# Gated linear attention with a feed-forward block: a chunk's 24 state products on four column groups instead of three

## The chip, the cores and the metric

The kernel runs on one core of a Trainium2 chip. The metric is the device time of one execution in microseconds. The core's engines are TensorE (PE, with its weight loads shown apart as PEld), VectorE (DVE), ScalarE (ACT), GpSimd (POOL), and SyncE (SP), which issues most of the transfers. TensorE's array can be used as four groups of 32 columns; a product in a group writes the 32 partitions of the accumulator (PSUM) that belong to the group.

## The reference

Everything is float32. First comes an attention block with complex gates, for 4 batches, 8 heads, 768 time steps and a head width of 48; then a feed-forward block over the 3072 rows that it leaves.

```python
mag = np.sqrt(a_re * a_re + a_im * a_im)
scale = np.minimum(mag, 0.999) / (mag + 1e-06)
a_re_n, a_im_n = (a_re * scale, a_im * scale)
for t in range(S):
    ar, ai = (a_re_n[:, :, t, :, None], a_im_n[:, :, t, :, None])
    new_re = ar * S_re - ai * S_im
    new_im = ar * S_im + ai * S_re
    kv = np.einsum('bhd,bhe->bhde', k[:, :, t], v[:, :, t])
    S_re, S_im = (new_re + kv, new_im)
    y[:, :, t] = np.einsum('bhd,bhde->bhe', q[:, :, t], S_re)
...
x = np.ascontiguousarray(attn_out.transpose(0, 2, 1, 3)).reshape(B * S, H * D)
a = x @ w1
b = x @ w2
h = a * b @ w3
return (h @ w_out).astype(np.float32)
```

## The kernel before

The product of w3 and w_out is formed once at the start (`fuse`), so the feed-forward block is two products with w1 and w2, their elementwise product `ab`, and one product with the fused matrix `w3o`.

The attention is cut into 8 units: 4 batches of two halves of 384 steps, each of three chunks of 128 steps, with all 8 heads in a unit. For each unit the gates are turned into running magnitudes and angles (on ScalarE and VectorE, tiles `gA`, `gR`, `gZ`, `re`, `im`), q and k are scaled and rotated by them, and the results are moved by transfers into `QL` and `KL`, whose partitions hold 96 rows per head (48 real, 48 imaginary). Then come, chunk by chunk:

- `turn` (L984): transposes of the scaled k on TensorE into `tp`, copied by ScalarE to `KT`. A chunk has two, for the real and the imaginary part.
- `state` (L1060): the state of 96 rows by 48 columns for each head, as a product of `KT` and v. The 96 rows are three blocks of 32, so a chunk has 8 heads times 3 blocks, 24 products, each with all 128 partitions in, 32 columns of weights and 48 columns moving. They stand in the tile `kv`, with block g of every head on column group g. The sum with the chunk before goes into a tile `T` (three of them take turns): one VectorE addition for all heads (L1075), or one ScalarE copy at a batch's first chunk (L1073). At the end of a unit's third chunk a second VectorE operation (L1078) multiplies the state by a gate. A batch needs five states, so 20 stages run in all: 4 with the copy and 16 with the addition.
- `scores` (L995): the products of `KL` and `QL` into two accumulator tiles `sc`, four column groups, with 128, 32, 96 and 64 columns; VectorE copies them with a mask into `A` (L1007).
- `outputs` (L1018): `A` with v, and `QL` with the state `T`, into `y`. From unit 2 on, `y` is split into three parts `x`, by ScalarE (L1047), VectorE (L1050) and POOL (L1051).

`tp`, `kv` and `y` share a pool of two accumulator tiles, `ps_v` (L464): a new one needs the one before last to be read out.

The feed-forward products of the unit before (`m` at L1089, `o` at L1184, evicted at L1101, L1105, L1123, L1130 and L1188) fill TensorE between these pieces. TensorE's order is written out by `pieces` (L1489) and `unit` (L1519). The gate steps of the next unit are placed between them on VectorE and ScalarE by a planner: `run` (L1579) keeps a clock for each engine, charges each piece of work by a table `TIMES` (L1536), and puts a step where it thinks that it fits. The first 36 places are fixed by a list (L441). The same clocks decide how many inspections of the raw inputs (`look`, from L1264: a load, then three to five operations on POOL) go ahead of the `x` operations in POOL's queue; the loads of the next unit's k, q and v stand behind the `x` operations in that queue. A fallback for unusual inputs, at the head of the file, isn't run here.

## Time and profile before

| what | us |
| --- | --- |
| three timed runs | 534.25, 535.98, 538.77 |
| their median | 535.98 |
| span of the profiled execution, first to last instruction (its only time on record) | 534.5 |
| a state stage's 48 records on TensorE, along the chain | 0.81 to 0.88 |
| addition of a state, L1075, mean of 16 | 0.549 |
| copy of a state, L1073, median of 4 | 0.466 |

The profile shows two records for each float32 product, so a stage of 24 products is "x48". Its rows by tile:

```profile
L1069 PEld LDWEIGHTS kv<-vr,KT x960: 106/110/110, 59.3 to 461.7; 128*32 128x32 f32 x192
L1069 PE MATMUL kv<-vr,KT x960: 206/206/231, 59.3 to 461.7; 128*32 128x48 f32 x192
L1073 ACT COPY T<-kv x4: 458/466/477, 61.2 to 396.7; 96x384 f32<-96x384 f32 x4
```

The columns are the shortest, median and longest duration in ns, the first and last start in us, and the form. A single record takes 206 ns from end to end, but a stage of 48 takes under 0.9 us, since records on different column groups overlap and successive ones are pipelined. A row of the page's groups has the line, engine, operation, output and inputs with their shapes and the count, then busy time, mean ns and idle time ahead of the engine. A row of a timeline or of the chain has its start and its length first. "x" after the tile names is a count; x as a name is the split output.

### The profile page before, as it was taken

How to read it: one execution, taken by the hardware profiler on the slowest of the kernel's cores; microseconds unless marked ns; L12 is line 12 of the kernel's file. 1: busy time of each engine (PE TensorE's matmuls, PEld its weight loads, DVE VectorE, ACT ScalarE, POOL GpSimd, SP SyncE). 2: the span in 40 equal slices, each digit the busy share in tenths (PEclk: the TensorE clock that was granted, in tenths of full speed). 3: DMA queues.
4: the chain of work that ended last, by engine and by line, in shares of the span. 5: the costliest groups of instructions: out<-in, count | busy, mean ns of one | idle time of the engine just before them, and what ended most of it. 6: DMA issues, size and time to landing. Idle time of an engine off the chain costs nothing.

```text
span 534.5 us, 13643 instructions
## 1 busy us (share of the span) xinstructions
PE 498.3 (93%) x5594; PEld 378.1 (71%) x5594; DVE 374.7 (70%) x607; ACT 325.6 (61%) x569; POOL 254.0 (48%) x317
## 2 busy tenths in 40 slices
PE   5689889999998999988999999999999998999995
PEld 2355565556655679957888688967896787878972
DVE  7999699855779988756773876577657837336750
ACT  6979866665675458982587557855786554213420
POOL 1000000028968886752664765487457458415510
PEclk9899999999999999998999999999999999999999
DMA  8999859692379219791599239932993176716611
GB/s 258 369 400 286 189 161 307 126 232 72 79 174 229 73 56 234 157 219 40 126 236 216 77 82 245 225 90 70 229 232 87 40 209 169 205 43 189 200 50 37
DMA packets 66424, 89.75 MB, mean 168 GB/s; under 512 B 29872, under 2 KB 53872, under 8 KB 65584
## 3 DMA queue, kind: packets, MB, share of 16 engines
q1 hardware_dynamic: 57904, 59.15, 44.0%
q0 software_dynamic: 8448, 29.63, 20.3%
q8 instruction: 46, 0.75, 0.6%
q14 instruction: 26, 0.21, 0.1%
HBM read 61.01 MB, written 4.72 MB: 123 GB/s over the span
## 4 chain that ended last, share of the span: by engine, by line
PE 51%; DVE 17%; DMA 13%; issue 6%; ACT 5%; POOL 5%; SPq 1%; POOLq 0%; DVEq 0%; ACTq 0%
PE m L1089 24%; PE o L1184 16%; PE y L1043 4%; PE sc L1004 4%; DMA k<-in_k_dram 3%; DMA KL<-k 3%; PE kv L1069 2%; DVE gR L750 2%; PE tp L991 2%; DMA QL<-q 2%; DMA q<-in_q_dram 2%; DMA look<-in_a_re_dram 1%; DVE gA L753 1%; DMA raw<-in_w_dram 1%; POOL look L1327 1%
## 5 line engine op out<-in xcount | busy, mean ns | idle before, releaser
L1184 PE MATMUL o<-w3o,ab 128*128 128x384 f32 x384 | 131.7, 492 | 0.0
L1089 PE MATMUL m<-x,low 128*128 128x384 f32 x576 | 119.2, 339 | 0.0
L1089 PEld LDWEIGHTS m<-x,low 128*128 128x128 f32 x576 | 102.6, 188 | 0.2 <-ACT m L1123 0.2
L1184 PEld LDWEIGHTS o<-w3o,ab 128*128 128x128 f32 x384 | 70.4, 190 | 45.6 <-issue 2.4
L1105 DVE TENSOR_TENSOR ab<-m,ab 128x384 f32<-128x384 f32 x64 | 35.1, 553 | 57.2 <-PE m L1089 39.4
L1089 PE MATMUL m<-x,wh 128*128 128x384 f32 x288 | 69.6, 350 | 3.4 <-ACT ab L1130 2.4
L1123 ACT ACTIVATE m<-m 128x384 f32<-128x384 f32 x96 | 45.5, 476 | 36.0 <-PE m L1089 35.6
L1089 PE MATMUL m<-xT,ws 128*128 128x384 f32 x192 | 63.1, 487 | 1.2 <-ACT xT L1054 1.2
L1328 POOL TENSOR_SCALAR look<-look 128x192 f32<-128x192 f32 (+1 forms) x55 | 54.4, 988 | 5.0
L1089 PEld LDWEIGHTS m<-x,wh 128*128 128x128 f32 x288 | 50.8, 188 | 7.4 <-ACT ab L1130 3.6
L1325 POOL TENSOR_TENSOR look<-look 128x256 f32<-128x256 f32 (+1 forms) x43 | 31.9, 743 | 50.1 <-DMA look<-in_w_dram 32.3
L1089 PEld LDWEIGHTS m<-xT,ws 128*128 128x128 f32 x192 | 36.0, 190 | 25.6 <-ACT xT L1054 1.7
L1273 POOL MEMSET seen<- 128x256 bf16 x1 | 0.3, 317 | 107.7 <-DVE ab L1105 107.7
L1007 DVE COPY_PREDICATED A<-mask,sc 128x512 f32<-128x512 uint8 x48 | 32.8, 734 | 26.5 <-PE sc L1004 26.5
L1289 POOL TENSOR_TENSOR seen<-seen,look 128x192 bf16<-128x192 bf16 (+1 forms) x55 | 44.3, 805 | 4.5
L1051 POOL TENSOR_TENSOR x<-x,x 128x384 fp32r<-128x384 f32 x18 | 23.1, 1284 | 41.7 <-DVE x L1050 41.5
L1188 ACT COPY ot<-o 128x384 f32<-128x384 f32 x24 | 11.4, 476 | 48.4 <-PE o L1184 48.2
L1043 PE MATMUL y<-A,V 128*32 128x128 f32 x768 | 40.2, 276 | 0.6 <-issue 0.6
L1004 PEld LDWEIGHTS sc<-QL,KL 96*32 96x32 f32 x1536 | 29.2, 112 | 13.6 <-issue 8.7
L1004 PE MATMUL sc<-QL,KL 96*32 96x32 f32 (+3 forms) x1536 | 32.8, 238 | 4.4 <-DMA QL<-q 3.0
L1043 PEld LDWEIGHTS y<-A,V 128*32 128x32 f32 x768 | 35.0, 112 | 1.5 <-issue 1.5
L1043 PE MATMUL y<-QL,T 96*32 96x128 f32 x640 | 35.6, 275 | 0.0
(163 smaller groups left out, 909.2 us busy)
## 6 DMA issues: line engine op xcount, KB each, us to landing
looked<-in_w_dram POOLq DMA_DIRECT2D x14, 512.0 KB, 4.5
look<-in_w_dram POOLq DMA_DIRECT2D x27, 256.0 KB, 5.0
raw<-in_w_dram SPq DMA_DIRECT2D x6, 1024.0 KB, 10.3
KL<-gR SPq DMA_DIRECT2D x24, 192.5 KB, 3.6
KL<-k SPq DMA_DIRECT2D x24, 192.5 KB, 7.1
QL<-gA SPq DMA_DIRECT2D x24, 192.0 KB, 8.2
QL<-q SPq DMA_DIRECT2D x24, 192.0 KB, 7.9
raw<-in_w_dram SPq DMA_DIRECT2D x6, 768.0 KB, 6.1
```

The lines of the kernel that those rows point to most:

```text
L1004: nc.tensor.matmul(out=sc[SB * g:SB * g + SB, j, s0:C], lhsT=KL[:, x * n + j, w][:, s0:s0 + SB], rhs=QL[:, x * n + j, w][:, s0:C], start=T ...
L1007: last["sc", u, c, x] = nc.vector.copy_predicated(out=A[:, x * n:(x + 1) * n], data=sc, mask=mask)
L1043: nc.tensor.matmul(out=o, lhsT=a, rhs=b, start=s0, stop=s1)
L1051: nc.gpsimd.tensor_tensor(out=x[2], in0=x[1], in1=x[0], op=OP.subtract)
L1089: nc.tensor.matmul(out=out, lhsT=a, rhs=b, start=start and i == 0, stop=i == len(terms) - 1, skip_group_check=not start)
L1105: last["ab", u, j] = nc.vector.tensor_tensor(out=ab_t[u][:, j], in0=m, in1=ab_t[u][:, j], op=OP.mult)
L1123: nc.scalar.activation(out=got[m], in_=got[m], func=AF.Copy, scale=1.0 + 1.0 / BITS)
L1184: nc.tensor.matmul(out=m, lhsT=ab_t[u][:, f, t * P:(t + 1) * P], rhs=w3o[:, f], start=(f == 0), stop=(f == KF - 1))
L1188: nc.scalar.copy(out=o, in_=m)
L1289: nc.gpsimd.tensor_tensor(out=seen[:, 0:n], in0=seen[:, 0:n], in1=x, op=OP.add)
L1325: tt(out=x, in0=x, in1=x, op=OP.mult)
L1328: ts(out=x, in0=x, scalar1=low, scalar2=None, op0=OP.is_ge)
```

## The change

`kv` gets all 128 partitions. Heads 0 to 5 keep their places on column groups 0 to 2. The six products of heads 6 and 7 (two heads by three blocks) go to the fourth group, partitions 96 to 127: head slots 0 and 1 there hold block 0 of heads 6 and 7, slots 2 and 3 hold block 1, slots 4 and 5 block 2. So the 24 products are issued as six times four. What is summed is the same; since the blocks of heads 6 and 7 now lie on other partitions than their rows of `T`, the sum is written as four operations: heads 0 to 5 on 96 partitions, and three of 32 partitions and two heads, each from partitions 96 to 127 into its block. The same holds for the ScalarE copies. The table `TIMES` gets new costs for these three kinds of piece.

```diff
-        kv = ps_v.tile([2 * D, H, D], FP, tag="v", name="kv")
-        for hd in range(H):
-            rows = KT[:, hd].rearrange("p d x f -> p (d x f)")
+        kv = ps_v.tile([P, H, D], FP, tag="v", name="kv")
+        fits, spare = H - H // LANES, 3 * SB
+        for hd in range(fits):
             for g in range(0, 2 * D, SB):
+                rows = KT[:, hd].rearrange("p d x f -> p (d x f)")
                 nc.tensor.matmul(out=kv[g:g + SB, hd], lhsT=rows[:, g:g + SB], rhs=V[:, hd], start=True, stop=True)
+            g, over = divmod(hd, H - fits)
+            rows = KT[:, fits + over].rearrange("p d x f -> p (d x f)")
+            nc.tensor.matmul(out=kv[spare:spare + SB, hd], lhsT=rows[:, SB * g:SB * g + SB], rhs=V[:, fits + over],
+                             start=True, stop=True)
         Tn = Tb[(u * UC + c) % 3]
+        areas = [(slice(0, 2 * D), slice(0, 2 * D), slice(0, fits), slice(0, fits))]
+        areas += [(slice(SB * g, SB * g + SB), slice(spare, spare + SB), slice(fits, H), slice(g * (H - fits), (g + 1) * (H - fits)))
+                  for g in range(3)]
         with tc.high_priority():
-            if T is None:
-                nc.scalar.copy(out=Tn[:, :, 0:D], in_=kv)
-            else:
-                nc.vector.tensor_tensor(out=Tn[:, :, 0:D], in0=kv, in1=T[:, :, 0:D], op=OP.add)
+            for rows, lanes, heads, slots in areas:
+                if T is None:
+                    nc.scalar.copy(out=Tn[rows, heads, 0:D], in_=kv[lanes, slots])
+                else:
+                    nc.vector.tensor_tensor(out=Tn[rows, heads, 0:D], in0=kv[lanes, slots], in1=T[rows, heads, 0:D], op=OP.add)
...
-        "tr": (("PE", 0.36), ("ACT", 0.85)), "kv0": (("PE", 0.89), ("ACT", 0.46)), "kv": (("PE", 0.89), ("DVE", 0.56)),
-        "rho": (("PE", 0.89), ("DVE", 1.1)), "sc": (("PE", 0.64), ("DVE", 0.74)), "y": (("PE", 1.87), ("ACT", 0.46)),
+        "tr": (("PE", 0.36), ("ACT", 0.85)), "kv0": (("PE", 0.72), ("ACT", 1.1)), "kv": (("PE", 0.72), ("DVE", 1.0)),
+        "rho": (("PE", 0.72), ("DVE", 1.55)), "sc": (("PE", 0.64), ("DVE", 0.74)), "y": (("PE", 1.87), ("ACT", 0.46)),
```

TensorE, the first state stage of unit 0, before: three transposes at a time into `tp`, then the stage's products as one row.

```order
L991 MATMUL tp<-ident,gR 128x128 x3
L991 MATMUL tp<-ident,k 128x128 x3
L991 MATMUL tp<-ident,gR 128x128 x3
L1069 MATMUL kv<-vr,KT 32x48 x24
L991 MATMUL tp<-ident,k 128x128 x3
```

And now; L1070 are the products of heads 0 to 5, L1073 those of heads 6 and 7.

```order
L991 MATMUL tp<-ident,gR 128x128 x3
L1070 MATMUL kv<-vr,KT 32x48 x3
L1073 MATMUL kv<-vr,KT 32x48
L1070 MATMUL kv<-vr,KT 32x48 x3
L1073 MATMUL kv<-vr,KT 32x48
L1070 MATMUL kv<-vr,KT 32x48 x3
L1073 MATMUL kv<-vr,KT 32x48
```

Nothing else moves on TensorE, here or later; after each three products one for the fourth group is issued, six times a stage.

VectorE, the second and third state of unit 0, before: `ws` and `low` are parts of the weights' conversion, `gA` is a gate step of unit 1, `A` the masked scores.

```order
L1253 ISA ws<-ws,low 128x1024
L1075 TENSOR_TENSOR T_123<-kv,T_122 96x8x48
L1236 TENSOR_SCALAR low<-raw 128x512
L1250 TENSOR_SCALAR ws<-raw 128x512
L824 SCALAR_TENSOR_TENSOR gA<-gZ,gA 128x3x384
L1253 ISA ws<-ws,low 128x1024
L1236 TENSOR_SCALAR low<-raw 128x256
L1075 TENSOR_TENSOR T_124<-kv,T_123 96x8x48
L1078 TENSOR_TENSOR T_124<-T_124,KL 96x8x48
L1007 COPY_PREDICATED A_90<-mask,sc_86 128x512
```

And now, with line numbers 3 to 9 higher.

```order
L1262 ISA ws<-ws,low 128x1024
L1084 TENSOR_TENSOR T_123<-kv,T_122 96x6x48
L1084 TENSOR_TENSOR T_123<-kv,T_122 32x2x48 x3
L1245 TENSOR_SCALAR low<-raw 128x512
L1259 TENSOR_SCALAR ws<-raw 128x512
L824 SCALAR_TENSOR_TENSOR gA<-gZ,gA 128x3x384
L1262 ISA ws<-ws,low 128x1024
L1245 TENSOR_SCALAR low<-raw 128x256
L1084 TENSOR_TENSOR T_124<-kv,T_123 96x6x48
L1084 TENSOR_TENSOR T_124<-kv,T_123 32x2x48 x3
L1087 TENSOR_TENSOR T_124<-T_124,KL 96x8x48
L1007 COPY_PREDICATED A_90<-mask,sc_86 128x512
```

The order is the same; each addition is four instructions, and all of them stand ahead of the masking of the scores.

From unit 2 on, the new costs make the planner place gate steps and evictions on VectorE and ScalarE a row or two earlier or later, and it puts nine inspections instead of eight ahead of the second set of `x` operations on POOL, and ten instead of nine ahead of the fourth; the last set has one fewer behind it.

## The prediction

> **What bounds the kernel now.** I read the page's busy shares and slices first, then TensorE's own waits after the start, then the chain that ended last, and last the timelines around the stages that the change touches.

> ```profile
> span 534.5 us, 13643 instructions
> PE 498.3 (93%) x5594; PEld 378.1 (71%) x5594; DVE 374.7 (70%) x607; ACT 325.6 (61%) x569; POOL 254.0 (48%) x317
> 60.00:110.00 50.00, 47.14 (x580) 30.90 (x571) 45.67 (x67) 35.26 (x51) 0.00 (x0) 1.00 0.75 192
> 273.00:487.00 214.00, 207.60 (x2713) 169.35 (x2711) 138.09 (x202) 124.48 (x231) 127.97 (x160) 1.00 0.62 151
> ```

> The last two rows are stretches (length, then busy time of PE, PEld, DVE, ACT, POOL). TensorE is the bound over most of the span: in the long steady stretch it is busy 207.6 of 214.0 us while VectorE has 138.1. Between 60 and 110 us VectorE is nearly as full as TensorE, 45.7 against 47.1 of 50.

> ```profile
> PE sc L1004 <- DMA QL<-q: 3.0, 1, 3.0
> PE kv L1069 <- ACT KT L993: 2.9, 2, 2.2
> PE tp L991 <- DVE T L1075: 0.2, 1, 0.2
> PE 51%; DVE 17%; DMA 13%; issue 6%; ACT 5%; POOL 5%; SPq 1%; POOLq 0%; DVEq 0%; ACTq 0%
> PE m L1089 24%; PE o L1184 16%; PE y L1043 4%; PE sc L1004 4%; DMA k<-in_k_dram 3%; DMA KL<-k 3%; PE kv L1069 2%; DVE gR L750 2%; PE tp L991 2%; DMA QL<-q 2%; DMA q<-in_q_dram 2%; DMA look<-in_a_re_dram 1%; DVE gA L753 1%; DMA raw<-in_w_dram 1%; POOL look L1327 1%
> ```

> The first three rows are the two longest and the last of eleven kinds of wait of TensorE from 68 us on (total, times, longest); together they are 15 us, and only 0.2 us of them is for a state sum on VectorE. The last two are the chain's shares. The state products (PE kv) hold 2% of 534.5 us, some 10.7 us, which is 13 of the 20 stages at the 0.8 us of the rows below. So a TensorE saving in a stage should mostly reach the end, and seven stages lie where another engine or a transfer sets the pace.

> **The change part by part: the products.** A step here is one product on each column group, moving 48 columns. A product is two records in the trace, so 24 products are 48 records: 16 steps of three before, 12 steps of four after. The price of a step comes from three stages on the chain:

> ```profile
> 169.01 0.88 PE kv L1069 x48
> 181.35 0.81 PE kv L1069 x48
> 186.28 1.25 PE sc L1004 x64
> 192.44 3.52 PE y L1043 x128
> 461.11 0.81 PE kv L1069 x48
> ```

> The kv rows shown stand for the 13. The scores (sc) are 16 steps on four groups with widths of 128, 96, 64 and 32 columns in equal number, 80 on average; kv is 16 steps on three groups with 48. Taking both as 16 steps at c per column plus a fixed start f: 16·80·c + f = 1.25 and 16·48·c + f = 0.81 give c = 0.86 ns and f = 0.15 us. The outputs (y) check it: 32 steps of 128 columns at 0.86 ns are 3.52 us, as measured, on four groups. So a step costs its width and not the number of groups, and the fourth group rides along. Four steps fewer are 4·48·0.86 = 165 ns. The lower bound is nothing, if the four weight loads of a step, not its columns, set the pace; the upper is a plain ratio, 0.81·4/16 = 0.20 us. I take 0.165, since the fixed start stays and sc and y already run four groups at that price. Over 20 stages it is 3.3 us, over the 13 on the chain 2.15 us.

> **The sums.** One VectorE addition of 96x384 becomes one of 96x288 and three of 32x96, 16 times; four times it is a ScalarE copy. No row has these sizes. The nearest:

> ```profile
> L1075 DVE TENSOR_TENSOR T<-kv,T 96x384 f32<-96x384 f32 x16 | 8.8, 549 | 12.1 <-PE kv L1069 12.1
> L944 DVE TENSOR_TENSOR gR<-k,gA 128x384 f32<-128x384 f32 x3 | 1.7, 553 | 0.0
> L962 DVE TENSOR_TENSOR gR<-k,re 128x1152 f32<-128x1152 f32 x1 | 1.4, 1359 | 2.1 <-ACT re L783 2.1
> L636 ACT ACTIVATE gZ<-gZ 128x384 f32<-128x384 f32 x12 | 6.1, 510 | 0.0
> L636 ACT ACTIVATE gZ<-gZ 128x768 f32<-128x768 f32 x12 | 10.0, 835 | 0.0
> 64.17 0.55 DVE L1075 TENSOR_TENSOR T<-kv,T 96x384 f32<-96x384 f32 x1
> 64.64 0.42 DVE L1236 TENSOR_SCALAR low<-raw 128x512 int32<-128x512 int32 x1
> ```

> Between 384 and 1152 elements VectorE takes (1359 − 553)/768 = 1.05 ns an element with 150 ns fixed. By that 96x288 is 0.45 us and each 32x96 is 0.25 us: 1.20 us end to end. But the next instruction starts 0.08 us before the addition ends (64.17 + 0.55 against 64.64), and the four parts don't depend on each other, so three such overlaps leave 0.96 us. The addition cost 0.55, so a stage gains 0.41 to 0.65 us of VectorE; I take 0.41, because these parts are independent as that pair was. The upper end holds if each waits for the one before. Over 16 stages it is 6.6 us, to 10.4 at most. ScalarE: (835 − 510)/384 = 0.85 ns an element and 0.185 us fixed make four parts 1.23 us against one of 0.51, so up to 0.7 us more per copy and 2.9 us over four; less with overlap.

> Whether that matters depends on what stands behind it. In the steady stretch a state is read again only in the next chunk's sum and, microseconds later, in y; a product tile goes back to its pool of two a little later, and only 0.2 us of TensorE's waits is for that. VectorE has 76 us spare of 214 there, so I cost those additions at nothing; without that cover they cost the 0.41 us each. One place has no cover, unit 0:

> ```profile
> 67.38 0.55 DVE L1075 TENSOR_TENSOR T<-kv,T 96x384 f32<-96x384 f32 x1
> 67.97 0.56 DVE L1078 TENSOR_TENSOR T<-T,KL 96x384 f32<-96x384 f32 x1
> 68.44 1.35 DVE L1007 COPY_PREDICATED A<-mask,sc 128x512 f32<-128x512 uint8 x2
> 69.22 1.40 PE L1004 MATMUL sc<-QL,KL 96*32 96x128 f32 x64 [0.62 <-DVE A L1007]
> 110.63 7.44 DMA look<-in_a_re_dram
> 144.58 8.10 DMA q<-in_q_dram
> ```

> VectorE works without a gap here, two additions (64.17, 67.38) stand ahead of the masking A in its queue, and TensorE waits for A. So 2·0.41 = 0.8 us lands on the path. It stays there: the chain goes on through VectorE to 110 us, and then through POOL's inspection of the inputs to the load of q. The savings of unit 0's three and unit 1's two stages are hidden under that and count nothing. The ScalarE copy of unit 0 lies in the same stretch, up to 0.7 us; I leave it out: it delays the next transposes and so the next product, and that one had time, since its sum started at 64.17 us, a microsecond after the end below. As upper bound it stays.

> ```profile
> 61.76 0.55 PE L991 MATMUL tp<-ident,gR 128*128 128x128 f32 x3 [0.41 <-ACT T L1073]
> 62.24 0.88 PE L1069 MATMUL kv<-vr,KT 128*32 128x48 f32 x48
> ```

> **The planner.** TensorE's order stays, but for the products themselves. On VectorE, ScalarE and POOL the gate steps and evictions of units 2 to 7 change places by one or two rows; I cost that at nothing, since nothing in the trace prices it, and the range carries it both ways. One part can be priced. POOL's queue gets one inspection group more ahead of two of the five sets of x products behind which the next loads stand: before the second set and before the fourth.

> ```profile
> 249.57 1.58 POOL L1051 TENSOR_TENSOR x<-x,x 128x384 fp32r<-128x384 f32 x1 [7.26 <-DVE x L1050]
> 354.95 0.59 POOL L1284 DMA_DIRECT2D look<-in_w_out_dram  x1 [0.30 <-POOL seen L1289]
> 358.48 0.59 POOL L1284 DMA_DIRECT2D look<-in_w_out_dram  x1 [0.30 <-POOL seen L1289]
> 361.63 1.60 POOL L1051 TENSOR_TENSOR x<-x,x 128x384 fp32r<-128x384 f32 x1 [0.18 <-DVE x L1050]
> 365.34 1.00 POOL L1051 TENSOR_TENSOR x<-x,x 128x384 fp32r<-128x384 f32 x1 [2.12 <-DVE x L1050]
> 367.56 1.65 POOL L1051 TENSOR_TENSOR x<-x,x 128x384 fp32r<-128x384 f32 x1 [1.22 <-DVE x L1050]
> 369.15 0.79 POOL L527 DMA_DIRECT2D k<-in_k_dram  x1
> ```

> A group takes 358.48 − 354.95 = 3.5 us. The first place has 7.26 us idle. The second has 0.18 + 2.12 + 1.22 = 3.5 us idle around the three x products, so the load of k stays where it is, just. Cost: 0, and 3.5 us if that cover is gone.

> **The sum.** −2.15 + 0.8 = −1.3 us on a profiled 534.5, so 533.2. The three timed runs have a median of 536.0 (534.25 to 538.77), 1.5 above the profiled span; on their footing I forecast 534.7 us, a saving below what a measurement can tell, which for this kernel is about 1%, or 5.4 us.

> **The rivals.**

> *The products gain nothing* (weight loads set the step, or each saving ends in the next wait): +0.8 alone, 536.8. For it: 15 us of waits remain on TensorE after 68 us. Against it: sc runs four groups at 0.86 ns per column.

> *All 20 stages count and unit 0's additions are hidden*: −3.3, so 532.7. Against it: TensorE's wait at 69.22 for A.

> *The additions become the bound, slower than before*: their own growth, 16·0.41 + 4·0.6 = 9 us, comes onto the path, as it does in unit 0: +9 − 2.15, so 542.8. It decides once more than 2.15 us of the 9 lands, that is, once five additions do instead of two. For it: 17% of the chain is VectorE. Against it: 76 us spare in the steady stretch. [...]

> *The extra inspection delays the k load*: +3.5 − 1.3, so 538.2.

> *The new order closes waits*: a third of the 15 us goes, −5 − 1.3, so 529.7. Nothing in the trace points at which.

> **Chances.** Forecast 0.55; products gain nothing 0.12; all stages 0.12; k load 0.07; additions bind 0.08; order closes waits 0.06. Only the last is faster by over 1% (below 530.6), with a little for the all-stages case on top: 0.07. Slower by over 1% (above 541.3) is the additions' case, 0.08. Within 1%: 0.85. The range runs over the four cases between and takes in the spread of the timed runs: 530.7 to 539.4; it leaves out the two outer cases, 0.14.

> **What would show it.** Products: a kv stage of 0.65 us instead of 0.81, while sc and y keep theirs; nearer 0.8 refutes the step price. Additions: about 0.45 us for 96x288 and 0.25 us for 32x96, starting 0.4 and 0.2 us apart; unit 0's A some 0.8 us later after its addition. Covers: TensorE's waits for T and A from 68 us on stay below a microsecond or two in total; the k load behind the fourth x set still follows its third x product at once. The forecast is wrong if TensorE's waits after 169 us grow by more than the 2.5 us that 15 stages save there, or if VectorE's queue is found full ahead of scores or evictions.

## The result, and the profile after

The changed kernel is slower: a median of 551.87 us (550.15 to 555.08, four runs) against 536.66 us (534.25 to 538.77, four runs) for the kernel before, a ratio of 1.027 with a 95% interval of 1.022 to 1.033. The forecast was 534.7 us and no change. The profiled execution took 555.08 us with a span of 553.2, 18.7 more than the span before.

The page of the changed kernel, its span and the busy time of each engine:

```profile
span 553.2 us, 13699 instructions
PE 505.6 (91%) x5594; PEld 383.2 (69%) x5594; DVE 387.9 (70%) x652; ACT 330.5 (60%) x581; POOL 260.3 (47%) x327
```

Two stretches of the same kernel (length, busy time of PE, PEld, DVE, ACT and POOL, then the granted clock):

```profile
60.00:110.00 50.00, 45.44 (x552) 29.88 (x553) 43.26 (x69) 32.24 (x49) 0.00 (x0) 0.93 0.69 180
273.00:487.00 214.00, 203.24 (x2423) 170.47 (x2423) 145.89 (x220) 137.09 (x255) 134.56 (x167) 0.97 0.65 157
```

No engine has become the bound. TensorE is busy for less of the steady stretch (203.2 us, it was 207.6) and gets through 2423 records in it, where it was 2713, at a mean clock of 0.97 where it was 1.00; VectorE has 68 us to spare. So TensorE waits more, and works more slowly for a part of the time. All its waits from 68 us on come to 25 us, where they were 15. Over the whole span the same 5594 records keep it busy for 7.3 us longer: between 57 us and the last stages its clock is at half for 30.7 us, where it was so for 3.4. Its waits from 68 us on, after the change (total, times, longest):

```profile
PE tp L991 <- DVE gR L750: 8.7, 5, 2.5
PE kv L1070 <- ACT KT L993: 4.8, 3, 3.7
PE sc L1004 <- DMA QL<-q: 3.2, 1, 3.2
PE sc L1004 <- DVE A L1007: 1.0, 2, 0.7
```

These are four of twelve kinds, and no wait for a state sum is left among the twelve. The wait that grew most is for `gR`, the last gate step ahead of a unit's first transposes. Before, it was:

```profile
PE tp L991 <- DVE gR L750: 1.6, 3, 0.7
```

TensorE at unit 4's first transposes before, in its timeline (start, length; in brackets the idle time ahead and what ended it):

```profile
274.99 0.27 PE L991 MATMUL tp<-ident,gR 128*128 128x128 f32 x1
275.93 0.44 PE L991 MATMUL tp<-ident,gR 128*128 128x128 f32 x2 [0.67 <-DVE gR L750]
```

And the same transposes after:

```profile
288.45 0.30 PE L991 MATMUL tp<-ident,gR 128*128 128x128 f32 x1 [1.85 <-DVE gR L750]
291.24 0.69 PE L991 MATMUL tp<-ident,gR 128*128 128x128 f32 x2 [2.48 <-DVE gR L750]
```

Why `gR` is late is seen some 40 us earlier on VectorE, in the chain of gate steps that ends in it. One early step of unit 4 is L653, whose result ScalarE needs at once. VectorE before:

```profile
235.49 0.55 DVE L653 SCALAR_TENSOR_TENSOR gA<-gZ,gA 128x384 f32<-128x384 f32 x1
235.97 0.55 DVE L1075 TENSOR_TENSOR T<-kv,T 96x384 f32<-96x384 f32 x1
```

VectorE after, up to the same step:

```profile
249.15 0.08 DVE L647 DVE_READ_ACCUMULATOR2_ANT st_tan<- 128x1 f32 x1
252.47 1.35 DVE L1007 COPY_PREDICATED A<-mask,sc 128x512 f32<-128x512 uint8 x2 [3.24 <-PE sc L1004]
254.63 0.74 DVE L1007 COPY_PREDICATED A<-mask,sc 128x512 f32<-128x512 uint8 x1 [0.81 <-PE sc L1004]
255.70 0.73 DVE L1007 COPY_PREDICATED A<-mask,sc 128x512 f32<-128x512 uint8 x1 [0.33 <-PE sc L1004]
256.32 1.41 DVE L653 SCALAR_TENSOR_TENSOR gA<-gZ,gA 128x384 f32<-128x384 f32 x2
```

And ScalarE after, the step that L653 reads and the step behind it:

```profile
245.38 0.62 ACT L636 ACTIVATE gZ<-gZ,consts 128x384 f32<-128x384 f32 x1
...
256.90 0.62 ACT L636 ACTIVATE gZ<-gA,consts 128x384 f32<-128x384 f32 x1 [6.70 <-DVE gA L653]
```

In the new order L653 stands behind four maskings `A` of unit 3. Those wait for unit 3's scores, so VectorE stands idle for 3.24 + 0.81 + 0.33 us with a step in its queue whose input was ready at 246.0 us (245.38 + 0.62). L653 comes 20.8 us later than before by the clock of the span, and 11 us later measured against TensorE's work at that place, which had slipped by 9.8.

TensorE's order is the same in both kernels, so its matmuls can be matched one by one; how much later each starts than its twin before shows where the time goes. Worked out as the median over the feed-forward and output products of a stretch, and given as what each unit adds (us; the start of unit 0 itself lies up to 1.0 us earlier or 0.3 us later than before, which counts only in the last column):

```
                     units 0,1  unit 2  unit 3  unit 4  unit 5  behind   at the end
changed kernel          4.3      3.2     4.0     5.7     4.7    -3.0       18.9
```

### The profile page after: what moved, and what is told of

It is laid out like the page before. It is cut to its first block, busy times and chain, and to the rows that moved or that the text cites. A ratio compares the mean times of both kernels' runs of the same rounds, so it can differ in the third digit from the quotient of the medians.

```text
span 553.2 us, 13699 instructions
## 1 busy us (share of the span) xinstructions
PE 505.6 (91%) x5594; PEld 383.2 (69%) x5594; DVE 387.9 (70%) x652; ACT 330.5 (60%) x581; POOL 260.3 (47%) x327
## 4 chain that ended last, share of the span: by engine, by line
PE 60%; DVE 14%; ACT 9%; DMA 7%; issue 5%; POOL 4%; SPq 0%; DVEq 0%; ACTq 0%; POOLq 0%
PE m L1098 24%; PE o L1193 18%; PE y L1043 6%; PE sc L1004 5%; PE f L1460 2%; DMA q<-in_q_dram 2%; PE tp L991 2%; PE kv L1070 1%; DMA im<-in_a_im_dram 1%; DMA QL<-q 1%; DVE low L1164 1%; DMA look<-in_a_re_dram 1%; DVE gR L750 1%; ACT re L636 1%; POOL look L1337 1%
## 5 line engine op out<-in xcount | busy, mean ns | idle before, releaser
L1098 PE MATMUL m<-x,low 128*128 128x384 f32 x576 | 122.6, 345 | 0.4 <-ACT m L1132 0.2
L1098 PEld LDWEIGHTS m<-x,low 128*128 128x128 f32 x576 | 105.2, 192 | 1.3 <-ACT m L1132 1.3
L1337 POOL TENSOR_SCALAR look<-look 128x256 f32<-128x256 f32 (+1 forms) x57 | 59.6, 1045 | 5.2
L1098 PEld LDWEIGHTS m<-x,wh 128*128 128x128 f32 x288 | 52.4, 192 | 3.4 <-ACT ab L1139 1.5
L1334 POOL TENSOR_TENSOR look<-look 128x256 f32<-128x256 f32 (+1 forms) x45 | 32.1, 714 | 45.7 <-DMA look<-in_w_dram 27.4
L1007 DVE COPY_PREDICATED A<-mask,sc 128x512 f32<-128x512 uint8 x48 | 32.8, 731 | 26.9 <-PE sc L1004 26.7
L1298 POOL TENSOR_TENSOR seen<-seen,look 128x256 bf16<-128x256 bf16 (+1 forms) x57 | 47.7, 837 | 4.7
L1051 POOL TENSOR_TENSOR x<-x,x 128x384 fp32r<-128x384 f32 x18 | 19.8, 1103 | 52.7 <-DVE x L1050 52.6
L1043 PE MATMUL y<-A,V 128*32 128x128 f32 x768 | 40.8, 279 | 1.6 <-issue 1.6
L1004 PEld LDWEIGHTS sc<-QL,KL 96*32 96x32 f32 x1536 | 29.4, 113 | 14.8 <-issue 11.1
L1004 PE MATMUL sc<-QL,KL 96*32 96x64 f32 (+3 forms) x1536 | 33.3, 239 | 5.4 <-DMA QL<-q 3.2
L1043 PEld LDWEIGHTS y<-A,V 128*32 128x32 f32 x768 | 35.1, 112 | 2.6 <-issue 2.5
L1043 PE MATMUL y<-QL,T 96*32 96x128 f32 x640 | 36.4, 280 | 0.0
```

What stands on the lines that cost most here:

```text
L1004: nc.tensor.matmul(out=sc[SB * g:SB * g + SB, j, s0:C], lhsT=KL[:, x * n + j, w][:, s0:s0 + SB], rhs=QL[:, x * n + j, w][:, s0:C], start=T ...
L1007: last["sc", u, c, x] = nc.vector.copy_predicated(out=A[:, x * n:(x + 1) * n], data=sc, mask=mask)
L1043: nc.tensor.matmul(out=o, lhsT=a, rhs=b, start=s0, stop=s1)
L1051: nc.gpsimd.tensor_tensor(out=x[2], in0=x[1], in1=x[0], op=OP.subtract)
L1098: nc.tensor.matmul(out=out, lhsT=a, rhs=b, start=start and i == 0, stop=i == len(terms) - 1, skip_group_check=not start)
L1298: nc.gpsimd.tensor_tensor(out=seen[:, 0:n], in0=seen[:, 0:n], in1=x, op=OP.add)
```

## The experiments

Theory A: the planner, given new costs, books the gate steps later, TensorE waits for `gR` and `KT`, and stretches at half clock follow. Theory B: the split sums themselves delay the readers of the state and of the product tile. The first three kernels keep the two apart. The planner's order doesn't depend on the products or the sums, only on `TIMES`, so each can be had without the other.

**The change with the old costs.** The three entries of `TIMES` are those of before.

```diff
-"kv0": (("PE", 0.72), ("ACT", 1.1)), "kv": (("PE", 0.72), ("DVE", 1.0)), "rho": (("PE", 0.72), ("DVE", 1.55))
+"kv0": (("PE", 0.89), ("ACT", 0.46)), "kv": (("PE", 0.89), ("DVE", 0.56)), "rho": (("PE", 0.89), ("DVE", 1.1))
```

> Change kept in full (four column groups, split sums), but the planner's cost rows put back to the values of before, so that every other instruction stands in the order of before. Theory A, the new order of the gate steps makes TensorE wait, and the stretches at half clock follow: the order of before returns, waits for gR and KT after 170 us fall back to about their sum before, and the time is 536 us plus at most the 4.2 us that unit 0 lost, so 534 to 541. Theory B, the split sums themselves delay the tile's readers: the loss stays, 548 to 553.

Measured: a ratio to the kernel before of 1.000 (0.996 to 1.003). The whole loss is gone with the products on four groups and the sums in four parts.

**The new costs alone**: the same three entries, put into the kernel before.

> The kernel before with nothing but the planner's three new cost rows: products on three groups, one sum each, the other instructions in the order of after. Theory A: the loss is here without the products and without the split sums, 546 to 552. Theory B: 535 to 538, as before. If both have a part, the two losses of this kernel and of the one with the old costs add up to about 15 us.

Measured: 1.028 (1.024 to 1.033). Not one instruction of the change is in this kernel, only the order, and it loses all that the change lost. Theory B falls, for the loss as a whole. TensorE's wait for `gR` in this kernel:

```profile
PE tp L991 <- DVE gR L750: 8.5, 5, 2.1
```

**The split sums alone**, on three groups and with the old costs:

```diff
+for rows, heads in [(slice(0, 2 * D), slice(0, 6))] + [(slice(SB * g, SB * g + SB), slice(6, H)) for g in range(3)]:
```

> The kernel before, its sums split in four parts as in after (heads 0 to 5, then 6 and 7 in three parts of 32 rows), products on three groups as before, old cost rows. Theory A: the split sums cost little where no wait is short, so 536 to 541, and unit 0 alone shows a longer wait for the state's copies. Theory B: 548 to 553. Against the kernel with the old costs it prices the products alone: 20 stages by 0.165 us, so 2 to 3 us longer than that one if the gain is on the chain.

Measured: 1.0035 (1.000 to 1.007), so 1.9 us with an uncertainty as large. Against the kernel with the old costs the products give 0.36% back, 1.9 us, again no more than the two intervals allow.

**The clock.** The changed kernel has stretches at half clock that the kernel before has not. Five pairs stand in its trace: a window at full clock in which TensorE worked little, then the half clock. The first, fourth and fifth pair (columns as above, PEclk after the five engines):

```profile
58.31:61.72 3.41, 1.27 (x52) 0.89 (x51) 1.43 (x2) 3.39 (x7) 0.00 (x0) 1.00 1.08 244
61.72:68.55 6.83, 6.17 (x101) 4.05 (x105) 6.22 (x13) 4.98 (x10) 0.00 (x0) 0.50 0.55 110
287.01:290.42 3.41, 0.30 (x1) 0.14 (x1) 2.24 (x4) 2.44 (x7) 2.72 (x4) 1.00 0.82 184
290.42:297.24 6.82, 6.00 (x20) 5.58 (x21) 6.63 (x7) 3.32 (x6) 4.89 (x7) 0.50 0.75 197
348.45:351.86 3.41, 0.99 (x5) 0.50 (x3) 2.54 (x4) 3.41 (x9) 2.63 (x3) 1.00 1.01 169
351.86:358.68 6.82, 5.16 (x18) 4.73 (x18) 6.28 (x8) 2.88 (x7) 5.56 (x6) 0.50 0.73 197
```

Is the half clock the loss, or does it go with it? Two kernels fill the waits of units 4 and 5.

```diff
+if u in (4, 5) and c == x == 0 and f < 2:
+    for _ in range((5, 10)[f]):
+        nc.tensor.matmul(out=tp[:, f:].rearrange("p f t -> p (f t)"), lhsT=ident, rhs=w3o[:, 0, C * f:], start=True, stop=True)
```

> The changed kernel with products whose results nothing reads put into two waits of TensorE (units 4 and 5, before the first transposes of gR: five of 384 columns and ten of 256). If the clock falls because the windows with these waits are too little busy, the stretches at half clock near 290 and 352 us go and the time falls by 4 to 8 us from 551.9. If the clock falls for another cause, the time stays or grows by up to 2 us. If the waits themselves and not the clock are the whole loss, it stays within 1 us.

Measured: 1.033 (1.030 to 1.037), a median of 555.7 us, above all that was expected. The two stretches at half clock were gone, but the added products were too many, as the next expectation says. The second kernel has `(3, 5)` in place of `(5, 10)`.

> As the kernel with idle products, with three of 384 columns and five of 256 in place of five and ten, since those ran 7.9 us where the two waits were 4.3, and so held the second transposes of gR up by 4.2 us themselves. If the granted clock follows how busy the window before was, the stretches at half clock near 290 and 352 us are gone and the waits are filled; TensorE worked some 11 us at half clock there, so the time falls by up to 5.6 us from that of after, to 546 to 549. If what comes behind waits for the gate steps and not for TensorE, the half clock goes and the time stays within 1.5 us of after.

Measured: 1.028 (1.020 to 1.036), as the change's 1.027. The timeline of TensorE in that kernel at unit 4, the added products in the first and third row:

```profile
286.03 2.10 PE L993 MATMUL tp<-w3o,ident 128*128 128x384 f32 x6
288.02 0.33 PE L995 MATMUL tp<-ident,gR 128*128 128x128 f32 x1
288.19 2.32 PE L993 MATMUL tp<-w3o,ident 128*128 128x256 f32 x10
291.14 0.44 PE L995 MATMUL tp<-ident,gR 128*128 128x128 f32 x2 [0.63 <-DVE gR L750]
...
294.73 0.44 PE L995 MATMUL tp<-ident,k 128*128 128x128 f32 x2 [0.74 <-DVE k L758]
```

And the granted clock there, a window and the stretch behind it:

```profile
287.00:290.41 3.41, 3.41 (x15) 2.26 (x13) 2.31 (x4) 2.03 (x6) 2.48 (x4) 1.00 0.85 180
290.41:297.24 6.83, 5.21 (x28) 4.31 (x28) 6.83 (x8) 4.04 (x8) 4.80 (x7) 1.00 0.71 191
```

With TensorE kept busy here (3.41 of 3.41 us, where it was 0.30 in the changed kernel) the clock stayed at 1.00, so the low activity is what took it down in this place. But the transposes stand where they stood, at 291.14 against 291.24, and at full speed TensorE is then held by the next gate step, `k`, for 0.74 us; in the changed kernel the same transposes of `k` came without a wait. VectorE is busy for all of those 6.83 us. By the matching of matmuls the two units win some 2 us in the profiled execution, out of 13.6 us at half clock, and the time of the runs doesn't show it, though its interval leaves room for it. In these two places the half clock is mostly a second effect of the late gate steps. The other three stretches of the changed kernel, 17.1 us in units 0 to 3, were not filled.

**Which part of the order: POOL's or VectorE's.** The planner moves both the inspections on POOL (theory A1, the prediction's own rival) and the gate steps (theory A2). Its constant `HOLD` moves the inspections alone.

```diff
-    HOLD, COSTS = 9.0, (4.9, 4.5, 6.8, 2.5)
+    HOLD, COSTS = 7.5, (4.9, 4.5, 6.8, 2.5)
```

> The kernel before with one number of its planner changed (HOLD 7.5 instead of 9.0), which puts the inspections on POOL and the loads behind them in the order of after, while VectorE's gate steps and ScalarE stay in the order of before. Theory A1, the inspection ahead of the third x and the load of k makes the gate's inputs late: 548 to 553, as with the new costs. Theory A2, the gate steps' own places on VectorE and ScalarE make them late: 535 to 540.

Measured: 1.002 (0.997 to 1.007). The reverse, the changed kernel with `HOLD` at 11.0:

> The changed kernel with HOLD 11 instead of 9.0: the inspections and loads on POOL stand within a few rows where they stood before, VectorE and ScalarE stay in the order of after. A1: 535 to 541, the loss is gone. A2: 548 to 553, the loss stays, and TensorE's waits for gR stay near 8.7 us in total.

Measured: 1.028 (1.019 to 1.036), and TensorE's wait for `gR` is

```profile
PE tp L991 <- DVE gR L750: 8.8, 5, 2.6
```

A1 falls, and A2 holds: the gate steps' places on VectorE and ScalarE carry the loss.

**Which cost.** The changed kernel with only the TensorE cost lowered, the sums' costs as before:

> The changed kernel with the planner's TensorE cost of the products lowered to 0.72, but the costs of the sums left as before (0.46, 0.56, 1.1). POOL's order is then that of after, the orders of VectorE and ScalarE are close to those of after. If the lowered product cost is what moves the gate steps: 547 to 553. If the raised costs of the sums do it: 535 to 541.

Measured: 1.018 (1.010 to 1.026). The lower price of the products alone loses some two thirds; the interval allows anything from 0.4 to nearly all. The planner places a gate step only if, by its own clocks, the step can start before TensorE's next item is over (`start(op) < bound`); what isn't placed by the time a unit's own products come is booked there, all at once. For L653 of unit 4 its clocks in the changed kernel have VectorE free at 204.15 against a bound of 204.05, then 204.89 against 204.69 and 205.63 against 205.43: refused by 0.1 to 0.2 us at three score pieces in a row, each of which puts another `A` ahead of it. Counted in that booking, the steps left over for units 3, 4 and 5 are 0, 5 and 5 in the kernel before, in the one with the old costs, with the split sums alone and with the inspections alone; they are 3, 14 and 14 in every kernel with the full loss and in this one. (These are numbers of the kernel's planner, not of the chip.) Three kernels set other counts. First, a TensorE cost halfway:

```diff
-"kv0": (("PE", 0.72), ("ACT", 1.1)), "kv": (("PE", 0.72), ("DVE", 1.0)), "rho": (("PE", 0.72), ("DVE", 1.55))
+"kv0": (("PE", 0.8), ("ACT", 0.46)), "kv": (("PE", 0.8), ("DVE", 0.56)), "rho": (("PE", 0.8), ("DVE", 1.1))
```

> The changed kernel with the planner's costs of the sums as before and a TensorE cost of the products halfway (0.80). By the planner's own booking, 3 gate steps of unit 3 are still unplaced when that unit's first products come, 14 of unit 4 and 5 of unit 5; before it was 0, 5 and 5, with the rows of after 3, 14 and 14. Theory, the steps left over are what TensorE waits for: the shift of unit 4's start is there (about 5 us) and that of unit 5's start is not, so 540 to 545 and a wait for gR in one unit only. Rival, any move of the order costs all of it: 547 to 553. Rival, the steps left over mean nothing: 535 to 538 or anything else that does not follow the units.

Measured: 1.021 (1.015 to 1.026), 548.5 us, above the 540 to 545 expected; the total lies where the rival put it, that any move of the order costs all. Then a TensorE cost above that of before, 1.0 in all three entries, with the sums' raised costs kept:

> The changed kernel with the raised costs of the sums kept (1.1, 1.0, 1.55) and a TensorE cost of the products above that of before (1.00). The planner then leaves 3, 5 and 5 steps for units 3, 4 and 5, though ScalarE's order differs from that of before in 299 rows of a comparison. Theory of the steps left over: 535 to 541, waits for gR no longer than 1 us each. Rival, the raised costs of the sums lose by themselves: 546 or more.

Measured: 1.009 (1.006 to 1.013), 543.5 us, again above what was expected and below the rival's 546; the waits for `gR` were 0.8 us in all, as expected. The totals were missed; unit by unit, in the table below, units 4 and 5 came out as the counts say, and unit 3 and those ahead of it didn't. The other two kernels change the rule itself and leave the costs alone.

```diff
-return start(op) < bound and start(op) + op[1] <= request(op[0], k) + slack
+return start(op) < bound + 0.2 and start(op) + op[1] <= request(op[0], k) + slack
```

> The changed kernel with its new costs and one tolerance added to the planner's rule: a gate step may start up to 0.2 us after TensorE's next item instead of not at all. By its booking 0, 1 and 4 steps of units 3, 4 and 5 are then left over, where after has 3, 14 and 14. Theory of the steps left over: the whole loss goes with the new costs still in place, 533 to 540, and TensorE's waits for gR fall under 3 us in total. Rival, the new costs themselves or any departure from the order of before loses: 545 or more (this order differs from that of before in 110 rows on VectorE and 312 on ScalarE).

> The kernel before, nothing of the change in it, with a tolerance of 0.1 us in the same rule. By its booking 6, 10 and 4 steps of units 3, 4 and 5 are then left over, where before has 0, 5 and 5. Theory of the steps left over: units 3 and 4 start late, unit 5 does not, 543 to 552. Rival, only the products, the sums or their costs can lose the time: 535 to 539.

Measured: the whole change with a tolerance of 0.2 us has 1.008 (1.003 to 1.013), so 0.8% instead of 2.7%; its 542.5 us lie above the 533 to 540 expected, while the waits for `gR` fell to 0.2 us. The kernel before with a tolerance of 0.1 us, with nothing of the change in it, has 1.029 (1.020 to 1.039); its 554.3 us lie above the 543 to 552 expected. The same table for all of these (what each unit adds in the profiled execution, against the kernel before; "left over" is the planner's count for units 3, 4, 5):

```
                          left over   units 0,1  unit 2  unit 3  unit 4  unit 5  behind   at the end
changed kernel            3, 14, 14      4.3      3.2     4.0     5.7     4.7    -3.0       18.9
new costs alone           3, 14, 14      2.3      6.2     3.7     4.9     4.7    -1.7       20.1
inspections put back      3, 14, 14      4.3      5.4     2.9     5.3     4.8    -2.8       19.8
product cost alone        3, 14, 14      1.6      0.5     3.1     4.4     4.5    -1.2       12.7
product cost 0.80         3, 14,  5      2.7      1.1     2.8     5.1    -0.2    -0.7       11.1
product cost 1.00         3,  5,  5      4.1      2.0     5.2    -0.4    -1.0    -0.1        9.7
before, tolerance 0.1     6, 10,  4      6.7      2.5     7.9     3.6     0.3     0.5       21.2
change, tolerance 0.2     0,  1,  4      4.1      1.7    -0.3     1.1     0.4     0.3        7.6
old costs                 0,  5,  5      2.2      1.9    -2.7     0.1    -0.3    -0.8       -0.5
```

In units 4 and 5 the time follows the count. Where 14 steps of a unit are left over it loses 4.4 to 5.7 us, with 10 it loses 3.6, with 5 or fewer at most 1.1. Unit 3 follows it less closely: three left over go with 2.8 to 5.2 us and six with 7.9. The -2.7 of the old costs in unit 3 goes with a stretch at half clock, 3.4 us long, that the kernel before has at 243 us and this one has not (a mean clock of 0.94 against 1.00 from 242 to 273 us). What the count does not explain stands in the first two columns: units 0 to 2 lose 2.1 to 9.7 us in the profiled executions. That holds with the old costs too, where the 4.1 us are made up later. The clock in the same traces goes with it: in units 0 and 1 the rows of this table with 6.8 us at half clock lose 4.1 to 6.7 us, and those with 3.4 us or none lose 1.6 to 2.7. No run fills the waits there, so whether the half clock is the cause in these units or again an effect isn't shown.

The kernel with tolerance 0.2 shows what else can be lost. It no longer waits for `gR` for long, but the two longest of its waits are for evictions of the feed-forward products:

```profile
PE m L1098 <- ACT ab L1139: 4.0, 4, 1.6
PE m L1098 <- DVE ab L1114: 3.6, 5, 1.6
```

In the kernel with the old costs the first of these is 2.4 us. A likely reason is that gate steps which may start late now hold up the evictions behind them; no run tests it.

**The sums, once more.** With the old costs and two sums in place of four:

```diff
-areas += [(slice(SB * g, SB * g + SB), slice(spare, spare + SB), slice(fits, H), slice(g * (H - fits), (g + 1) * (H - fits)))
-          for g in range(3)]
+areas += [(slice(0, 2 * D), slice(0, 2 * D), slice(fits, H), slice(0, H - fits))]
```

> The change with the planner's costs of before, and two sums in place of four: the second adds heads 0 and 1's products to the state of heads 6 and 7 in one part of 96 rows and 96 columns, so the state of heads 6 and 7 is left out, and what is timed is the change with two sums less in each of the 20 stages. If the small sums lie beside other work, as the prediction has it, this is the same as with four sums within 0.3%. If VectorE's 16 stages times two sums of some 0.26 us each were on the path, it is 3 to 8 us faster, 529 to 534.

Measured: 0.999 (0.994 to 1.003), the same as with four. Most of the small sums lie beside other work; the interval leaves room for a loss of some 2 us, which unit 0 does show (below).

**Versions to beat both.** Four groups only where VectorE adds:

```diff
-fits, spare = H - H // LANES, 3 * SB
+fits, spare = (H if T is None else H - H // LANES), 3 * SB
...
+    if T is None:
+        continue
```

> Planner's costs of before; products on four groups with four sums in the 16 stages whose sums VectorE adds, but three groups and one whole copy in the four stages where ScalarE copies (units 0, 2, 4 and 6 begin a state). If the four copies are what makes unit 0 late (1 to 2 us in the kernels that have them), this is 1 to 2 us faster than the kernel with the old costs and ends at 534 to 537, at or just under before. If not, it is the same within 0.3%.

Measured: 0.997 (0.994 to 1.0005), a median of 537.03 us against 538.51 for the kernel before beside it. It is the fastest kernel of the study, but the interval just includes no change. Units 0 and 1 add 2.3 us in its profiled execution as with the four copies (2.2), so the copies are not most of what makes them late. The same with the tolerance:

> A version to beat both: four groups and four sums in VectorE's 16 stages, three groups and a whole copy in ScalarE's four, the costs 0.72, 1.0 and 1.55 for the VectorE stages and those of before for the copies, and a tolerance of 0.3 us (0, 1 and 1 steps left over in units 3 to 5). If fewer steps left over than in before (0, 5, 5) shorten the waits it still has, 530 to 535; if TensorE's other waits take their place, 535 to 538, as the kernel with whole copies and the old costs.

Measured: 1.010 (1.006 to 1.015), a median of 542.1 us, above both ranges. Fewer steps left over than before did not help: the waits for `gR` are gone from the long ones, but those for the masking `A` are 4.4 us (1.2 before) and those for `ab` 4.2 us on ScalarE and 3.6 on VectorE (2.4 and 0.8 before).

## Why the prediction was wrong

**The step that failed** is the planner's: "the gate steps and evictions of units 2 to 7 change places by one or two rows; I cost that at nothing, since nothing in the trace prices it, and the range carries it both ways". It was +15 us. The premise was off already: between the traces of the kernel before and of the new costs alone, 227 of 604 instructions on VectorE and 323 of 569 on ScalarE stand at another place in the order, by up to 7 and 9 places, and L653 of unit 4 by five, one sum and four maskings. What counts is what it moved past: the maskings wait for another unit's scores, and the steps behind L653 are a chain, each on one engine waiting for one on the other. Of its 11 us TensorE's waits for `gR` ahead of unit 4 show 1.85 + 2.48. The range carried nothing for it: a rival "the new order closes waits" was priced at −5 us, and its other side, that it opens them, was not. The rows to bound it were there: before, TensorE already waited 1.6 us for `gR`, so `gR` had no time to spare, and a pair of maskings takes 1.35 us plus the wait for its scores. And the sign could have been had from the code alone, since the planner's count of steps left over went from 0, 5, 5 to 3, 14, 14.

**The products**: right, to the size of a stage's saving. A whole stage on TensorE's timeline before, the one that the chain shows from 181.35 on:

```profile
181.28 0.88 PE L1069 MATMUL kv<-vr,KT 128*32 128x48 f32 x48
```

The first and the last group of products of a stage after the change, at full clock:

```profile
480.13 0.24 PE L1070 MATMUL kv<-vr,KT 128*32 128x48 f32 x3
...
480.64 0.21 PE L1073 MATMUL kv<-vr,KT 128*32 128x48 f32 x1
```

From the first start to the last end a stage took 0.88 us before, all 20 of them, and takes 0.72 now, all 17 that ran at full clock: 0.16 us less, where 0.165 was forecast. The prediction's 0.81 is a chain row, which leaves out the first 0.07 us, so its sign (0.65 for 0.81) has to be read as 0.72 for 0.88. Its check by the outputs left out the fixed 0.15 us, with which 32 steps come to 3.67 us and not to the measured 3.52; the price held all the same. What reached the end, 1.9 us between two kernels, agrees with the 2.15 but is not resolved.

**The sums**: the size was wrong. The sums on VectorE and ScalarE in the changed kernel, and one stage's four:

```profile
L1084 DVE TENSOR_TENSOR T<-kv,T x64: 257/261/454, 64.5 to 482.0; 32x96 f32<-32x96 f32 x48, 96x288 f32<-96x288 f32 x16
L1082 ACT COPY T<-kv x16: 232/233/395, 61.2 to 419.6; 32x96 f32<-32x96 f32 x12, 96x288 f32<-96x288 f32 x4
```

```profile
480.91 1.33 DVE L1084 TENSOR_TENSOR T<-kv,T 96x288 f32<-96x288 f32 x4
```

The single durations came out as forecast (0.454 and 0.26 us for 0.45 and 0.25). But the four run end to end: 454 + 3·260 ns is 1.23 us of the 1.33. The 16 stages take 1.26 to 1.33 us, 0.71 to 0.78 more than the 0.55 before, not the 0.41 taken for the overlap of independent parts, and above the upper end of 0.65. That the parts are independent didn't decide it. In the changed kernel each starts 0.01 to 0.03 us after the one ahead has ended. In the kernel with the split sums alone the first small sum, which like the large one starts at partition 0, starts 0.08 us before the large one ends, and the next two, which start at 32 and 64, start 0.03 us after. Whether the partition is the reason, no run tests. That it costs little at the end was right: 0.35% (0 to 0.7%) by the kernel with the split sums alone. The rival in which the additions become the bound would have made this the loss; the kernel with the old costs, at 1.000, is against it. (The rival's own count was off by one: five additions at 0.41 are 2.05 us, so it takes six to pass 2.15.)

**Unit 0**: 0.8 us was put on two additions, with ScalarE's copies left out. The copies did show first, ScalarE and then TensorE after the change:

```profile
61.18 1.15 ACT L1082 COPY T<-kv 96x288 f32<-96x288 f32 x4
```

```profile
62.38 0.90 PE L991 MATMUL tp<-ident,gR 128*128 128x128 f32 x3 [1.10 <-ACT T L1082]
```

The wait was 0.41 us before. The sign that the prediction named, A some 0.8 us later after its addition, came out: before, A started 68.44 − 67.38 = 1.06 us after the last addition did, and now it starts 1.90 us after:

```profile
68.88 1.28 DVE L1084 TENSOR_TENSOR T<-kv,T 96x288 f32<-96x288 f32 x4
70.19 0.55 DVE L1087 TENSOR_TENSOR T<-T,KL 96x384 f32<-96x384 f32 x1
70.78 1.37 DVE L1007 COPY_PREDICATED A<-mask,sc 128x512 f32<-128x512 uint8 x2
```

But that is one addition of two. From unit 0's first transposes to its first A the traces have 11.8 us in the four kernels with whole sums, 13.6 in the two with split sums and whole copies, and 13.7 to 14.2 in those with four groups and everything split. So the two additions cost 1.8 us on the path there, and the copies up to 0.6, where 0.8 stood in the sum. That is about what the split sums alone lose at the end (1.9 us). What else makes units 0 to 2 later from execution to execution stays open.

**The inspection**: right. The fourth set of `x` on POOL and the load of `k` behind it, after the change:

```profile
382.40 1.01 POOL L1051 TENSOR_TENSOR x<-x,x 128x384 fp32r<-128x384 f32 x1 [2.67 <-DVE x L1050]
387.98 2.27 POOL L1051 TENSOR_TENSOR x<-x,x 128x384 fp32r<-128x384 f32 x2 [4.57 <-DVE x L1050]
390.19 0.79 POOL L527 DMA_DIRECT2D k<-in_k_dram  x1
```

The load still follows the third operation at once, and the inspections alone cost nothing that is measured. The prediction's own sign of failure was met: it named a growth of TensorE's waits after 169 us by over 2.5 us, and the one for `gR` alone grew by 7.1, all of them together by 8.7 (11.9 to 20.6).

## What to carry to other kernels

A cost table that a planner reads is part of the kernel: a more truthful cost for one piece can reorder work that has nothing to do with it, so a change and its new costs should be tried apart, and the planner's own count of steps that found no place should be compared first. A wait that is short in the profile means that the chain behind it has no time to spare at its end, not that it has no price: ask what a step queued one place later would stand behind. A stretch at half clock next to a wait can be a second effect of it (here the kernel with filled waits had 1.028 and the change 1.027); fill the wait and see whether the time moves.

## What the runs showed of the hardware

In the profiled execution two stretches of half clock, 13.6 us in all, were worth some 2 us; with the waits filled, VectorE was busy for 6.83 of 6.83 and 6.39 of 6.70 us in the two places.

Three independent 32x96 additions behind a 96x288 one did not overlap in the changed kernel (each started 0.01 to 0.03 us after the end of the one ahead), though a 0.55 us addition and the conversion behind it, before, did by 0.08 us.
